# Soft mixture tail of a fused kernel: four-chunk logit blocks, squares on two engines, six weight buffers, a chain in halves

## Chip, cores and metric

One core of a Trainium2 chip runs the whole program once. The metric is device time in microseconds (us), the median over runs. Engines are named as the profile names them: PE does matrix multiplies, DVE, ACT and POOL work elementwise, SP issues the data transfers (DMA). All transfers of this kernel go through one queue, SP's.

## The reference, cut to what matters

```python
attn = clustered attention over q, k, v          # [4, 8, 768, 64], 16 clusters
x = attn rearranged to [3072, 512]               # tokens x model
h = x @ w_in                                     # 512 -> 2048
x = (h * cos(h)) @ w_out                         # 2048 -> 512
logits = x @ phi                                 # 32 slots, 8 experts x 4
d = softmax(logits, axis=0); slot_input = d.T @ x
for e in 8 experts:
    slot_out[e] = relu(slot_input[e] @ w1[e]) @ w2[e]     # w1 [8,512,1024], w2 [8,1024,512]
c = softmax(logits, axis=1); out = c @ slot_out  # [3072, 512]
```

The expert weights w1 and w2 are 16.8 MB each in float32, and the output is 6.3 MB.

## The kernel before

The program has three stages, written out in one fixed order; each engine works through its own list in that order.

**Attention** (up to about 505 us) is not touched.

**MLP loop.** The 3072 tokens are 24 tiles of 128. A tile has four chunks of 512 hidden columns, so there are 96 chunks (`NC_`); the last two tiles are interleaved, so that the four buffers of `w_in` (pool `wbig`) come free one by one. Iteration c of the loop issues, in this order: `hchunk(c)`, twelve matmuls into `h` (L138); `post2(c-2)`, a sine on ACT (L751), its square on DVE (L755) and the product `gg` on DVE (L756); `post1(c-1)`, a copy on ACT (L145) and two range-reduction steps on DVE (L146, L147); `gev(c-4)`, a copy of the transposed chunk on ACT (L768); `gtr(c-3)`, four transposes on PE (L763). `h` has three buffers, so `hchunk(c)` waits for the product `gg` of chunk c-3. In odd iterations PE also does `logit` for two chunks (`lp`, L786; w_out is folded into `phi` beforehand, as `wphi`). Once a tile is complete its logits are copied (`soft1`), summed and spread (`lf`, L802 and L804), and their running maximum is taken on DVE (L808, L809); ACT loads the exponential's table (L824), takes the exponentials and loads the sine's table again (shown at L751); later `dt` (L850) and `accp` (L862) add the tile's weighted sum to `acc`.

**Tail.** After chunk 95 come the last logits, maximum, exponentials, `accp` and `acc` (L871), then `acct` (transposes of `acc`), `si` (times w_out, tiles `wo0` and `wo1`, L983), `sit` (L990), `he` (first expert layer, `expert_in`, L1006), `htp` (transposes), `so` (second expert layer, `expert_out`, L1051), `fo` (the output, L1071) and ten output transfers (L1081). `ctstack` builds the combine weights `ctk` in the tail. `warm` issues matmuls on a tile of zeros whose result nobody reads.

**Weights.** w1 and w2 are cut into 16 pieces of 2.1 MB: 0 to 7 are w1, 8 to 15 are w2 (8 to 11 for output columns 0 to 255, 12 to 15 for the rest, so that each contiguous run of a w2 piece is 256 floats, 1 KB; of a w1 piece it is 4 KB). Pool `wk` has five buffers: `wo0`, `wo1` and pieces 0 to 2, loaded in the MLP loop at c = 28, 36 and 44. Pieces 3 to 6 go to the four `wbig` buffers as `w_in` is used up (c = 89, 91, 93, 95), piece 7 and part of piece 8 to pool `wx`, opened when the MLP's buffers are closed. The rest follows as buffers come free: second half of 9 after the first half of `si`, 10 after `si`, 11 to 15 each after one step of `expert_in`. A load that has to wait for its buffer holds up all transfers written behind it on SP.

Of the kernel before, what the change touches and what calls it, by code (L numbers as in the profile page):

```python
# [19 lines left out]
P = 128  # L20
# [6 lines left out]
def clustered_attention_then_soft_moe(  # L27
# [64 lines left out]
    R = {}  # L92
# [22 lines left out]
    def xprep2(t):  # L115
# [3 lines left out]
        lo = mx.tile([P, DT, P], F32R, tag="xlo", name=f"xlo{t}", bufs=3)  # L119
# [589 lines left out]
    wk = ctx.enter_context(tc.tile_pool(name="wk", bufs=5))  # L709
# [14 lines left out]
    def load_part(n, e, w):  # L724
        SP.dma_start(out=w if n < 8 else w.rearrange("p (t d) -> p t d", t=4), in_=piece(n)[:, e])
        W.setdefault(n, {})[e] = w

    def load_piece(n, pool, tag):
        w = pool.tile([P, 4, 1024], F32, tag=tag, name=f"w{n}")
        if n < 8:  # L730
            SP.dma_start(out=w, in_=piece(n))
            W[n] = [w[:, e] for e in range(4)]
        else:
            for e in range(4):
                load_part(n, e, w[:, e])

    with ExitStack() as m:
        mp = m.enter_context(tc.tile_pool(name="m2", bufs=2))
# [3 lines left out]
        zero = mp.tile([P, GRP * P], BF16, tag="zero", name="zero", bufs=1)  # L742
        POOL.memset(zero, 0.0)
        wo = [wk.tile([P, 8, DM], F32, tag="wk", name=f"wo{x}") for x in range(2)]

        def post2(c):
# [5 lines left out]
            if c == NC_ - 2:  # L752
# [36 lines left out]
        def soft1(ts):  # L789
            n = len(ts)  # L790
            lps = mp.tile([P, n * P], F32, tag="lps", name=f"lps{ts[0]}", bufs=1)
# [24 lines left out]
        def softx(ts):  # L816
# [5 lines left out]
            d = mp.tile([P, n * P], F32, tag="d", name=f"d{ts[0]}", bufs=1)  # L822
            e = mp.tile([P, n, NS], F32, tag="e", name=f"e{ts[0]}")
# [10 lines left out]
        def soft3(ts):  # L834
# [37 lines left out]

        xsched = {}
# [12 lines left out]
        WARM = {96: 2, 97: 2, 98: 2, 99: 4, 100: 12, 101: 8, 102: 4}  # L886
        for c in range(2, NC_ + 8):
            if c < NC_:
# [241 lines left out]
```

## Time and profile before

| what | value |
|---|---|
| median of 3 runs | 975.82 us (973.89 to 977.09) |
| the profiled execution's own time | 976.18 us |
| its span, first to last instruction | 974.5 us |
| PE busy, share of the span | 94% |
| DVE busy | 82% |
| ACT busy | 65% |
| POOL busy | 48% |

The span is what the trace's clock covers; the profiled execution's time is 1.7 us more. A busy share is an average over stages with different limits, so the stages have to be read apart.

### The profile page before, as it was taken

To read this page: it belongs to the slowest core of one execution; us is meant where nothing else is said; L and a number is where in the kernel's file an instruction comes from. 1 tells how busy PE (TensorE), PEld (TensorE's weight loads), DVE (VectorE), ACT (ScalarE), POOL (GpSimd) and SP (SyncE) were. 2 spreads that over 40 slices of the span, in tenths; PEclk is the share of its full clock that TensorE was granted. 3 is DMA by queue.
4 is the path that set the end of the run, shared out by engine and by line. 5 is a ranking of instruction groups with operands and counts; after the bars stand their busy time and mean duration, and the time that the engine had idled before them with its cause. 6 is when DMAs were issued, how large, how long until landed. Compare 5 with 4: busy or idle time off the path is not lost.

```text
span 974.5 us, 16981 instructions
## 1 busy us (share of the span) xinstructions
PE 915.4 (94%) x5974; PEld 622.9 (64%) x5974; DVE 796.1 (82%) x1577; ACT 633.8 (65%) x1368; POOL 464.1 (48%) x342
## 2 busy tenths in 40 slices
PE   5899999999999999999998999999999999999895
PEld 3466656666655666556666777777777777666443
DVE  6789999989989898899887888888888888777141
ACT  4687777777777777777554666666666666566232
POOL 3547877777777778777862222222222222220000
PEclk9999999999999999999999999999999999999998
DMA  8968766688666886666230224331301010127999
GB/s 174 210 166 191 189 157 176 163 205 194 141 178 161 197 193 148 173 159 175 80 97 29 65 88 130 109 100 54 130 23 44 23 44 23 43 89 283 352 349 332
DMA packets 138628, 142.18 MB, mean 146 GB/s; under 512 B 58376, under 2 KB 113968, under 8 KB 138544
## 3 DMA queue, kind: packets, MB, share of 16 engines
q1 hardware_dynamic: 138544, 141.11, 54.0%
q8 instruction: 47, 0.77, 0.3%
q14 instruction: 37, 0.30, 0.1%
HBM read 86.27 MB, written 17.06 MB: 106 GB/s over the span
## 4 chain that ended last, share of the span: by engine, by line
PE 63%; DVE 15%; DMA 9%; ACT 7%; issue 3%; SPq 1%; POOL 1%; ACTq 0%; POOLq 0%; DVEq 0%
PE h L138 19%; PE o L411 10%; PE sm L364 6%; PE s L398 5%; PE s L399 5%; DVE mc L366 3%; PE gt L763 3%; DMA mds<-mrow 2%; DVE kk L755 2%; PE accp L862 2%; DMA st<-mds 2%; DMA w<-in_moe_w_out_dram 2%; PE lp L786 2%; DVE w L469 2%; PE he L1006 1%
## 5 line engine op out<-in xcount | busy, mean ns | idle before, releaser
L138 PE MATMUL h<-wc,xhi 128*128 128x512 f32 x768 | 250.0, 406 | 8.5 <-DVE gg L756 8.5
L419 POOL TENSOR_TENSOR ps<-ps,a 128x768 f32<-128x768 f32 x120 | 230.8, 1923 | 43.9 <-ACT wphi L504 23.8
L366 DVE TENSOR_REDUCE mc<-sm 128x1 f32<-128x384 f32 x384 | 202.9, 549 | 33.6 <-PE sm L364 31.9
L402 ACT ACTIVATE a<-s 128x384 f32<-128x384 f32 x384 | 173.5, 490 | 37.5 <-PE s L399 32.4
L138 PEld LDWEIGHTS h<-wc,xhi 128*128 128x128 f32 x768 | 137.2, 188 | 62.7 <-DVE kk L147 17.3
L398 PE MATMUL s<-st 97*128 97x384 f32 x384 | 141.3, 368 | 11.4 <-DMA st<-mds 10.0
L138 PE MATMUL h<-wc,xlo 128*128 128x512 f32 x384 | 151.6, 395 | 0.0
L364 PE MATMUL sm<-st 96*128 96x384 f32 x384 | 140.4, 391 | 8.9 <-DVE mc L366 5.1
L411 PE MATMUL o<-a,vt 128*64 128x384 f32 x768 | 145.1, 499 | 0.0
L399 PE MATMUL s<-st 128*128 128x384 f32 x384 | 130.0, 339 | 0.0
L751 ACT ACTIVATE kk<-kk 128x512 f32<-128x512 f32 x96 | 60.6, 632 | 80.7 <-DVE kk L147 80.4
L364 PEld LDWEIGHTS sm<-st 96*128 96x128 f32 x384 | 72.7, 193 | 55.1 <-DVE mc L366 28.5
L755 DVE TENSOR_TENSOR kk<-kk 128x512 f32<-128x512 f32 x94 | 78.2, 832 | 29.8 <-ACT kk L751 29.7
L398 PEld LDWEIGHTS s<-st 97*128 97x128 f32 x384 | 73.0, 190 | 29.8 <-issue 13.9
L411 PEld LDWEIGHTS o<-a,vt 128*64 128x64 f32 x768 | 47.8, 136 | 61.0 <-issue 55.5
L109 POOL TENSOR_TENSOR xn<-xn,rc 128x512 f32<-128x512 f32 x24 | 31.9, 1328 | 107.7 <-DMA rc<-recs 104.7
L138 PEld LDWEIGHTS h<-wc,xlo 128*128 128x128 f32 x384 | 72.2, 188 | 17.0
L416 POOL TENSOR_TENSOR ps<-a,a 128x768 f32<-128x768 f32 x30 | 54.8, 1825 | 39.7 <-ACT a L402 39.0
L121 POOL TENSOR_TENSOR xlo<-xn,xhi 128x512 fp32r<-128x512 f32 x24 | 36.5, 1523 | 77.6 <-DVE xhi L120 77.6
L399 PEld LDWEIGHTS s<-st 128*128 128x128 f32 x384 | 73.1, 190 | 0.0
L113 POOL TENSOR_TENSOR xn<-xn,rc 128x512 f32<-128x512 f32 x24 | 32.3, 1345 | 81.2 <-DVE rc L111 76.1
L756 DVE SCALAR_TENSOR_TENSOR gg<-kk,h 128x512 f32<-128x512 f32 x96 | 65.9, 687 | 4.5 <-POOL kk L755 1.1
(203 smaller groups left out, 1567.0 us busy)
## 6 DMA issues: line engine op xcount, KB each, us to landing
w<-in_moe_w_dram SPq DMA_DIRECT2D x8, 2048.0 KB
st<-qhi SPq DMA_DIRECT2D x32, 384.0 KB
st<-khi SPq DMA_DIRECT2D x64, 192.0 KB
w<-in_moe_w_dram SPq DMA_DIRECT2D x24, 512.0 KB
w<-in_moe_w_out_dram SPq DMA_DIRECT2D x16, 512.0 KB
w<-in_moe_w_in_dram SPq DMA_DIRECT2D x16, 512.0 KB
qt<-in_q_dram SPq DMA_DIRECT2D x32, 192.0 KB
kt<-in_k_dram SPq DMA_DIRECT2D x32, 192.0 KB
```

The lines of the kernel that those rows point to most:

```text
L138: PE.matmul(h, lhsT=x[:, d, :], rhs=wc[f][:, w, d, :], start=(n == 0), stop=(n == 3 * DT - 1))
L364: PE.matmul(m[:, 0:QW], lhsT=st[0:96, Q1 + h, qt * P:(qt + 1) * P], rhs=st[0:96, K1 + h, half * QW:(half + 1) * QW], start=True, stop=True)
L366: DVE.tensor_reduce(out=s["mc"][:, col:col + 1], in_=m[:, 0:QW], op=ALU.max, axis=AX.X)
L398: PE.matmul(x[:, 0:QW], lhsT=st[0:97, K1 + h, ks], rhs=st[0:97, Q1 + h, qs], start=True, stop=False)
L399: PE.matmul(x[:, 0:QW], lhsT=st[:, K2 + h, ks], rhs=st[:, Q2 + h, qs], start=False, stop=True)
L402: ACT.activation(out=T[i][u][:, h, :], in_=x[:, 0:QW], func=AF.Exp, scale=scale)
L411: PE.matmul(s["o"][64 * h:64 * h + 64, 0:QW], lhsT=s["v"][:, h, kt, :], rhs=t[:, h, :], start=(kt == 0), stop=(kt == KT - 1))
L416: (DVE if i == NPAIR - 1 else POOL).tensor_tensor(out=ps, in0=s[u - 1], in1=t, op=ALU.add)
L419: (DVE if i == NPAIR - 1 else POOL).tensor_tensor(out=ps, in0=ps, in1=t, op=ALU.add)
L751: ACT.activation(out=r, in_=r, func=AF.Sin, scale=0.5)
L755: (POOL if c == NC_ - 3 else DVE).tensor_tensor(out=r, in0=r, in1=r, op=ALU.mult)
L756: DVE.scalar_tensor_tensor(out=R["g", t][:, f * 512:(f + 1) * 512], in0=r, scalar=0.5, in1=h, op0=ALU.subtract, op1=ALU.mult)
```

## The change

In the MLP loop the logits of a tile are now computed in one block of four chunks, in every fourth iteration; the copied chunks have four buffers for it (pool `gsp`). The square is taken on ACT for even chunks and stays on DVE for odd ones. The tile `xlo` has two buffers where it had three, and some small tiles share buffers.

Pool `wk` has six buffers, so pieces 0 to 3 are loaded inside the loop (c = 28, 36, 44, 52) and `wbig` takes pieces 4 to 7. Pieces 8 to 11 are cut otherwise: all 512 output columns of the first four experts, 256 rows each, in runs of 4 KB; 12 to 15 are as before. After the first half of `si` a buffer is loaded with the second half of piece 9 and the first of 10, and so on (`load_halves`).

The code from chunk 95 on is written out by hand. The last chunk's copy is on DVE; the sum for `acc` of tile 21 and the table load stand elsewhere; the two logit results have banks of their own; `accp`, `acc`, `acct`, `si` and `sit` are done in halves of 256 columns; `ctstack` is split into `ct_dve`, `ct_pe` and `ct_ev`, whose four blocks stand between the steps of this chain instead of between the steps of `expert_out`. The second group's transposes (`expert_tr(1)`) stand behind piece 11.

```diff
-        lo = mx.tile([P, DT, P], F32R, tag="xlo", name=f"xlo{t}", bufs=3)
+        lo = mx.tile([P, DT, P], F32R, tag="xlo", name=f"xlo{t}", bufs=2)
...
-    wk = ctx.enter_context(tc.tile_pool(name="wk", bufs=5))
+    wk = ctx.enter_context(tc.tile_pool(name="wk", bufs=6))
...
-        hf, g, fq = (n - 8) // 4, (n - 8) // 2 % 2, n % 2
-        return w2[4 * g:4 * g + 4, 512 * fq:512 * fq + 512, 256 * hf:256 * hf + 256].rearrange("e (p t) d -> p e t d", p=P)
+        if n < 12:
+            y = n - 8
+            return w2[0:4, 256 * y:256 * y + 256, :].rearrange("e (p t) d -> p e t d", p=P)
+        hf, fq = divmod(n - 12, 2)
...
+    def load_halves(n, w):
+        for e in range(2):
+            load_part(n, 2 + e, w[:, e])
+        if n < 15:
+            for e in range(2):
+                load_part(n + 1, e, w[:, 2 + e])
...
+        gs_stack = ExitStack()
+        gsp = gs_stack.enter_context(tc.tile_pool(name="gsp", bufs=4))
...
-            if c == NC_ - 2:
+            if c == NC_ - 2 or (c % 4 in (0, 2)):
                 ACT.activation(out=r, in_=r, func=AF.Square)
...
-        def gev(c):
-            s = mp.tile([P, 512], F32, tag="gts", name=f"gts{c}", bufs=2)
-            ACT.activation(out=s, in_=R.pop(("gp", c)), func=AF.Copy)
+        def gev(c, eng=None):
+            s = gsp.tile([P, 512], F32, tag="gts", name=f"gts{c}")
+            if eng is DVE:
+                DVE.tensor_copy(s, R.pop(("gp", c)))
+            else:
+                ACT.activation(out=s, in_=R.pop(("gp", c)), func=AF.Copy)
...
+        def ct_dve(b):
+            cs = spare[:, 0:4 * KT * NS].rearrange("p (t a b s) -> p t a b s", t=KT, a=2, b=2)
+            eb = ck[:, b * KT:b * KT + KT, :].rearrange("p t (o s) -> p t o s", o=1).to_broadcast([P, KT, 2, NS])
+            DVE.tensor_copy(cs[:, :, :, 0, :], eb)
+            DVE.tensor_tensor(out=cs[:, :, :, 1, :], in0=eb, in1=cs[:, :, :, 0, :], op=ALU.subtract)
+
+        def ct_pe(b):
+            cf = spare[:, 0:4 * KT * NS].rearrange("p (t s) -> p t s", t=KT).bitcast(F32)
+            for x in range(2):
+                g = psum.tile([P, 512], F32, tag=("m0", "m3")[x], name=f"ctk{b}_{x}")
+                for y in range(3):
+                    PE.transpose(g[:, y * P:(y + 1) * P], cf[:, 3 * x + y, :], ident)
+                R["ct", b, x] = g
+
+        def ct_ev(b):
+            for x in range(2):
+                ACT.activation(out=ctk[:, b * KT + 3 * x:b * KT + 3 * x + 3, :],
+                               in_=R.pop(("ct", b, x))[:, 0:3 * P].rearrange("p (t s) -> p t s", t=3), func=AF.Copy)
...
-        WARM = {96: 2, 97: 2, 98: 2, 99: 4, 100: 12, 101: 8, 102: 4}
...
-            if c % 2 == 1 or c - 4 == NC_ - 1:
-                for x in (c - 5, c - 4):
-                    if 0 <= x < NC_ and ("gt", x) in R:
-                        logit(x)
+            if c % 4 == 3:
+                for x in range(max(c - 7, 0), c - 3):
+                    logit(x)
...
-            if c in (28, 36, 44):
...
+            if c in (28, 36, 44, 52):
                 load_piece((c - 28) // 8, wk, "wk")
...
-                load_piece(NF - 1 - (NC_ - 1 - c) // GRP + 3, wbig, "wbig")
...
-                load_piece(7, wx, "wx")
...
+                load_piece(NF - 1 - (NC_ - 1 - c) // GRP + 4, wbig, "wbig")
+
+        last = groups[-1]
+        post1(NC_ - 1)
+        post2(NC_ - 2)
+        post2(NC_ - 1)
+        gev(NC_ - 4)
+        gtr(NC_ - 3)
+        gev(NC_ - 3)
+        gtr(NC_ - 2)
+        logit(NC_ - 4)
+        logit(NC_ - 3)
+        mx_stack.close()
+        wx = ctx.enter_context(tc.tile_pool(name="wx", bufs=1, side="right"))
+        w8 = wx.tile([P, 1024], F32, name="w8b")
+        load_part(8, 2, w8)
+        cbuf = wx.tile([P, 3840], F32R, name="cbuf")
+        ctk = cbuf[:, 0:NT * P].rearrange("p (t s) -> p t s", t=NT)
+        spare = cbuf[:, NT * P:]
+        gev(NC_ - 2)
+        ACT.activation(out=ones[:, 0:1], in_=ones[:, 0:1], func=AF.Exp)
+        gtr(NC_ - 1)
+        gev(NC_ - 1, DVE)
+        soft5([NT - GRP - 1])
+        ct_dve(0)
+        warm(2)
+        logit(NC_ - 2)
+        logit(NC_ - 1)
+        gs_stack.close()
+        w9 = ctx.enter_context(tc.tile_pool(name="tail", bufs=1)).tile([P, 2, 1024], F32, name="w9a")
+        for e in range(2):
+            load_part(9, e, w9[:, e])
+        lps = mp.tile([P, GRP * P], F32, tag="ld", name="lpsz", bufs=1)
+        ACT.activation(out=lps, in_=R["lpg"].rearrange("p a b -> p (a b)"), func=AF.Copy)
+        warm(4)
...
+        DVE.tensor_reduce(out=mn, in_=lf, op=ALU.max, axis=AX.X)
+        DVE.tensor_scalar(out=ng, in0=mn, scalar1=R["m"], scalar2=-1.0, op0=ALU.max, op1=ALU.mult)
+        DVE.tensor_reduce(out=rn, in_=lt, op=ALU.max, axis=AX.X)
+        DVE.tensor_scalar(out=rn, in0=rn, scalar1=-1.0, scalar2=None, op0=ALU.mult)
+        R["soft2"] = lf, lt, R["m"], ng, rn
+        softx(last)
+        ct_pe(0)
+        ct_dve(1)
+        soft3b(last)
+        softe(last)
+        soft3a(last)
+        DVE.tensor_scalar(out=ssum, in0=ssum, scalar1=1e-9, scalar2=None, op0=ALU.add)
+        DVE.reciprocal(ssum, ssum)
+        ct_ev(0)
+        cr, dts = R["dts"]
+        ap = [psum.tile([P, 256], F32, tag=("v", "m1")[h], name=f"apz{h}") for h in range(2)]
+        gz = [R.pop(("g", t)) for t in last]
+        for h in range(2):
+            for y in range(GRP):
+                for j in range(4):
+                    PE.matmul(ap[h][32 * j:32 * j + 32, :], lhsT=dts[:, y * P + 32 * j:y * P + 32 * j + 32],
+                              rhs=gz[y][:, j * 512 + 256 * h:j * 512 + 256 * h + 256], start=(y == 0), stop=(y == GRP - 1))
         gl = ggp.tile([P, 2, 1024], F32, tag="gg", name="gl")
         load_part(8, 3, gl[:, 0])
         htb = ggp.tile([P, 2, 8, P], F32, tag="gg", name="htb")
...
+        for h in range(2):
+            x = slice(256 * h, 256 * h + 256)
+            DVE.scalar_tensor_tensor(out=acc[:, x], in0=acc[:, x], scalar=cr, in1=ap[h], op0=ALU.mult, op1=ALU.add)
+            g = psum.tile([P, 512], F32, tag="s", name=f"acct{h}", bufs=3)[:, 0:256]
+            for j in range(2):
+                PE.transpose(g[:, j * P:(j + 1) * P], acc[:, 256 * h + j * P:256 * h + (j + 1) * P], ident)
+            ACT.activation(out=acct[:, 2 * h:2 * h + 2, :], in_=g.rearrange("p (a b) -> p a b", a=2), func=AF.Copy, scale=-2.0)
+            if h == 0:
+                ct_pe(1)
+        soft3c(last)
+        ct_ev(1)
+        ct_dve(2)
+        si = [psum.tile([P, 256], F32, tag=("m2", "m1")[h], name=f"si{h}") for h in range(2)]
+        for xh in range(2):
+            for h in range(2):
+                for x in range(2 * xh, 2 * xh + 2):
+                    for f in range(4):
+                        PE.matmul(si[h][32 * f:32 * f + 32, :], lhsT=acct[:, x, 32 * f:32 * f + 32],
+                                  rhs=wo[xh][:, 4 * (x - 2 * xh) + f, 256 * h:256 * h + 256], start=(x == 0), stop=(x == 3))
...
+        def sit_half(h):
+            ACT.activation(out=sis[:, 256 * h:256 * h + 256], in_=si[h], func=AF.Copy, scale=ssum)
+            g = psum.tile([P, 2 * NS], F32, tag="v", name=f"sit{h}")
+            for d in range(2):
+                PE.matmul(g[:, d * NS:(d + 1) * NS], lhsT=sis[:, (2 * h + d) * P:(2 * h + d + 1) * P], rhs=gmat[:, 0, :], start=True, stop=True)
+            ACT.activation(out=sit[:, 2 * h:2 * h + 2, :], in_=g.rearrange("p (a b) -> p a b", a=2), func=AF.Copy)
+
+        sit_half(0)
+        ct_pe(2)
+
+    if True:
+        for n in (9, 10):
+            load_halves(n, wk.tile([P, 4, 1024], F32, tag="wk", name=f"wh{n}"))
...
+                if n == 0:
+                    sit_half(1)
+                    ct_ev(2)
+                    ct_dve(3)
                 if n < 5:
-                    load_piece(11 + n, *pools[n])
+                    pool, tag = (wk, "wk") if n < 4 else (wbig, "wbig")
+                    load_halves(11 + n, pool.tile([P, 4, 1024], F32, tag=tag, name=f"wh{11 + n}"))
...
+        expert_ev(0)
+        expert_in(1)
+        ct_pe(3)
         expert_tr(0)
-        expert_in(1)
-        cbuf = wbig.tile([P, 4096], F32R, tag="wbig", name="cbuf")
-        ctk = cbuf[:, 0:NT * P].rearrange("p (t s) -> p t s", t=NT)
...
+            if n < 12:
+                steps = [(hf, 2 * (n - 8) + t, 512 * t + 256 * hf) for t in range(2) for hf in range(2)]
+            else:
+                hf, fq = divmod(n - 12, 2)
...
+        for n in range(8, 12):
+            expert_out(n)
+        expert_tr(1)
+        expert_out(12)
+        expert_out(13)
...
+                expert_out(14, [x // 3])
...
+        expert_out(15)
```

On PE, one tile's worth of the loop, with the twelve matmuls of each `hchunk` left out (`gt`: transposes of a chunk, `lp`: logits, `dt` and `accp`: the weighted sum of the tile before). Before:

```order
L763 MATMUL gt_6925<-ident,gg_6775 128x128 x4
L786 MATMUL lp_6930<-gts_6870,wphi 32x128 x4
L786 MATMUL lp_6930<-gts_6909,wphi 32x128 x4
...
L763 MATMUL gt_6970<-ident,gg_6775 128x128 x4
L850 MATMUL dt_6975<-ident,d_6914 128x128
...
L763 MATMUL gt_7006<-ident,gg_6952 128x128 x4
L786 MATMUL lp_6930<-gts_6960,wphi 32x128 x4
L786 MATMUL lp_6930<-gts_6999,wphi 32x128 x4
L862 MATMUL accp_7021<-gg_6613,dts_6977 32x512 x4
```

After:

```order
L771 MATMUL gt_6928<-ident,gg_6768 128x128 x4
...
L771 MATMUL gt_6964<-ident,gg_6768 128x128 x4
L868 MATMUL dt_6969<-ident,d_6917 128x128
...
L771 MATMUL gt_7000<-ident,gg_6946 128x128 x4
L797 MATMUL lp_7005<-gts_6872,wphi 32x128 x4
L797 MATMUL lp_7005<-gts_6912,wphi 32x128 x4
L797 MATMUL lp_7005<-gts_6954,wphi 32x128 x4
L797 MATMUL lp_7005<-gts_6993,wphi 32x128 x4
L880 MATMUL accp_7024<-gg_6606,dts_6971 32x512 x4
```

The eight `lp` instructions that stood alone two iterations ahead of `accp` now stand directly ahead of the other eight.

On SP, the transfers from the last w_in buffer's release to the outputs (`w_...` and `wh_...`: whole buffers; `w8a`, `w8b`, `gl`, `w9a`: half and quarter pieces in other tiles). Before:

```order
L731 DMA w_10294<-in_moe_w_dram 128x4x1024
L731 DMA w_10376<-in_moe_w_dram 128x4x1024
L731 DMA w_10464<-in_moe_w_dram 128x4x1024
L725 DMA w8a<-in_moe_w_dram 128x4x256 x2
L731 DMA w_10544<-in_moe_w_dram 128x4x1024
L731 DMA w_10590<-in_moe_w_dram 128x4x1024
L725 DMA w8b<-in_moe_w_dram 128x4x256
L725 DMA gl<-in_moe_w_dram 128x4x256
L725 DMA w9a<-in_moe_w_dram 128x4x256 x2
L725 DMA w9b<-in_moe_w_dram 128x4x256 x2
L725 DMA w_10734<-in_moe_w_dram 128x4x256 x4
```

After:

```order
L733 DMA w_10291<-in_moe_w_dram 128x4x1024
L733 DMA w_10382<-in_moe_w_dram 128x4x1024
L733 DMA w_10457<-in_moe_w_dram 128x4x1024
L728 DMA w8a<-in_moe_w_dram 128x1024 x2
L733 DMA w_10550<-in_moe_w_dram 128x4x1024
L728 DMA w8b<-in_moe_w_dram 128x1024
L728 DMA w9a<-in_moe_w_dram 128x1024 x2
L728 DMA gl<-in_moe_w_dram 128x1024
L728 DMA wh_10764<-in_moe_w_dram 128x1024 x4
L728 DMA wh_10769<-in_moe_w_dram 128x1024 x4
L728 DMA wh_10793<-in_moe_w_dram 128x1024 x2
L728 DMA wh_10793<-in_moe_w_dram 128x4x256 x2
```

One whole buffer (`w_10590`, piece 7 in `wx`) is gone from this stretch, `w9a` stands ahead of `gl`, and the loads of pieces 8 to 11 are one run of 1024 per partition instead of four of 256.

## Rows read from the trace of the kernel before

**Rows 1.** Stretches: us; each engine's busy us (instructions); granted PE clock; DMA share; GB/s.

```profile
554.90:893.60 338.70, 333.37 (x2266) 253.21 (x2262) 287.39 (x642) 217.74 (x439) 83.30 (x60) 1.00 0.25 80
893.60:917.40 23.80, 19.79 (x178) 11.68 (x178) 8.47 (x23) 10.45 (x25) 1.04 (x1) 1.00 0.99 354
917.40:957.40 40.00, 38.29 (x424) 18.74 (x424) 11.50 (x53) 13.41 (x26) 0.00 (x0) 1.00 1.09 349
957.40:974.50 17.10, 6.57 (x52) 4.42 (x52) 3.19 (x5) 4.84 (x10) 0.00 (x0) 0.82 0.93 320
```

**Rows 2.** Chain that ended last, in the MLP loop: start us, us, what.

```profile
554.07 0.86 PE accp L862 x8
...
577.95 0.57 PE lp L786 x16
578.53 2.98 PE h L138 x12
...
582.05 2.80 PE h L138 x12
...
585.86 0.86 PE accp L862 x8
...
892.59 1.00 PE accp L862 x8
```

**Rows 3.** Waits of PE, 505 to 897 us: us in total, times, longest.

```profile
PE h L138 <- DVE gg L756: 8.5, 14, 1.1
```

**Rows 4.** Chain that ended last, in a tile where PE waits.

```profile
660.90 1.08 DVE kk L755
```

**Rows 5.** Groups: the square on DVE: count, busy us, mean ns, idle before.

```profile
L755 DVE TENSOR_TENSOR kk<-kk 128x512 f32<-128x512 f32 x93 | 77.5, 834 | 29.8 <-ACT kk L751 29.7
```

**Rows 6.** ACT in order of time: a sine and its one square.

```profile
897.11 0.62 ACT L751 ACTIVATE kk<-kk 128x512 f32<-128x512 f32 x1
897.76 0.63 ACT L753 ACTIVATE kk<-kk 128x512 f32<-128x512 f32 x1
```

**Rows 7.** Chain that ended last, from the last logits to the first expert layer.

```profile
902.55 0.43 PE lpg L786 x8
...
904.55 2.18 PE warm L884 x20
...
907.42 1.97 PE accp L862 x16
...
909.41 0.75 DVE acc L871
...
911.56 3.69 PE si L983 x32
...
917.45 7.12 PE he L1006 x64
```

**Rows 8.** SP's transfers in order of time: start us, us until the last was issued.

```profile
896.61 5.00 SPq L731 DMA_DIRECT2D w<-in_moe_w_dram  x2
...
908.55 0.55 SPq L725 DMA_DIRECT2D gl<-in_moe_w_dram  x1
...
915.26 35.12 SPq L725 DMA_DIRECT2D w<-in_moe_w_dram  x24
```

**Rows 9.** Stretches as in rows 1, cut by which weights were on their way.

```profile
871.30:896.60 25.30, 24.89 (x172) 18.25 (x171) 17.43 (x40) 16.80 (x35) 1.04 (x1) 1.00 0.73 265
...
900.00:908.00 8.00, 6.99 (x80) 4.75 (x76) 2.38 (x9) 4.53 (x13) 0.00 (x0) 1.00 1.02 409
...
925.00:955.00 30.00, 29.02 (x341) 15.66 (x343) 11.50 (x53) 12.31 (x25) 0.00 (x0) 1.00 1.10 349
```

**Rows 10.** Chain that ended last: the last weight transfer.

```profile
948.96 8.47 DMA w<-in_moe_w_dram
```

**Rows 11.** PE in order of time: six transposes, early and a little later.

```profile
5.47 1.51 PE L249 MATMUL tpq<-ident,qt 128*128 128x128 f32 x6 [0.90 <-DMA qt<-in_q_dram]
...
35.38 0.85 PE L249 MATMUL tpk<-ident,kt 128*128 128x128 f32 x6 [0.54 <-DMA kt<-in_k_dram]
```

More of the change, by code (lines that the diff above doesn't have):

```diff
@@ L729, in load_piece @@
         w = pool.tile([P, 4, 1024], F32, tag=tag, name=f"w{n}")
[L730 to L735, printed above, removed]
+        SP.dma_start(out=w, in_=piece(n))
+        W[n] = [w[:, e] for e in range(4)]
+    def load_halves(n, w):
[4 more added lines that the diff above has]
+                load_part(n + 1, e, w[:, 2 + e])
     with ExitStack() as m:
-        mp = m.enter_context(tc.tile_pool(name="m2", bufs=2))
+        mp = ctx.enter_context(tc.tile_pool(name="m2", bufs=2))
         m0 = mp.tile([P, 1], F32, tag="mrun", name="mrun")
@@ L944, in clustered_attention_then_soft_moe @@
                 x = (c - 12) // 8
[L945 to L946 removed]
+                for y in range(2):
+                    SP.dma_start(out=wo[x][:, 4 * y:4 * y + 4], in_=wod.rearrange("(f y p) d -> y p f d", f=4, p=P)[2 * x + y])
+            if c in (28, 36, 44, 52):
                 load_piece((c - 28) // 8, wk, "wk")
[L948 removed]
+            if NC_ - GRP * NF <= c and (NC_ - 1 - c) % GRP == 0:
                 if c == NC_ - 1:
@@ L963, in clustered_attention_then_soft_moe @@
         htb = ggp.tile([P, 2, 8, P], F32, tag="gg", name="htb")
-    with ExitStack() as z:
-        tp = z.enter_context(tc.tile_pool(name="tail", bufs=1))
-        w9 = tp.tile([P, 2, 1024], F32, name="w9a")
-        for e in range(2):
-            load_part(9, e, w9[:, e])
-        pools = [(wk, "wk")] * 3 + [(wbig, "wbig")] * 2
-        DVE.tensor_scalar(out=ssum, in0=ssum, scalar1=1e-9, scalar2=None, op0=ALU.add)
-        DVE.reciprocal(ssum, ssum)
-        g = mbank("acct")
-        for j in range(4):
-            PE.transpose(g[:, j * P:(j + 1) * P], acc[:, j * P:(j + 1) * P], ident)
-        acct = wphi.rearrange("p a s -> p (a s)").rearrange("p (a b) -> p a b", a=4)
-        ACT.activation(out=acct, in_=g.rearrange("p (a b) -> p a b", a=4), func=AF.Copy, scale=-2.0)
-        g = mbank("si")
-        for f in range(4):
-            for j in range(4):
-                ft = 4 * f + j
-                PE.matmul(g[32 * j:32 * j + 32, :], lhsT=acct[:, j, 32 * f:32 * f + 32], rhs=wo[ft // 8][:, ft % 8, :],
-                          start=(f == 0), stop=(f == 3))
+        acct = wphi.rearrange("p a s -> p (a s)").rearrange("p (a b) -> p a b", a=4)
@@ L985, in clustered_attention_then_soft_moe @@
         hs = gl[:, 1]
         sis = hs[:, 0:512]
-        ACT.activation(out=sis, in_=g, func=AF.Copy, scale=ssum)
-        g = mbank("sit")
-        for d in range(DT):
-            PE.matmul(g[:, d * NS:(d + 1) * NS], lhsT=sis[:, d * P:(d + 1) * P], rhs=gmat[:, 0, :], start=True, stop=True)
         sit = phis
-        ACT.activation(out=sit, in_=g[:, 0:DT * NS].rearrange("p (a b) -> p a b", a=DT), func=AF.Copy)
-        w9 = wk.tile([P, 4, 1024], F32, tag="wk", name="w9b")
-        for e in range(2, 4):
-            load_part(9, e, w9[:, e])
```

120 lines of the change are left out of this document (47 added, 73 removed).

## Prediction

> **What bounds the kernel now.** I read the stretches first [rows 1]. In the MLP loop PE is busy 333 of 339 us, DVE 287 and ACT 218, while the transfers run at 80 GB/s: PE sets the pace there. From 893.6 us on it is the other way round: the transfers run at 354 and 349 GB/s with a DMA share of 0.99 and 1.09, up to the last weight, and the outputs follow at 320. So the end of the kernel is set by when the MLP loop ends and by how many bytes are still to move then, and at what rate.
>
> In the loop, the chain of waits [rows 2] runs over PE through most tiles: `h`, transposes, `lp`, `accp`. From the `accp` of tile 0 (554.07) to that of tile 21 (892.59, itself 0.14 us longer) 21 tiles take 338.5 us, 16.1 each. The tile between 570.0 and 585.86 has no wait in its chain and takes 15.87. The difference comes from waits: PE stands 8.5 us in all, 14 times, because `gg` of three chunks back is late [rows 3], always after the softmax of a tile, where two table loads hold up the sine; then the chain runs sine, square, `gg`, `h` (such a square in [rows 4]).
>
> In the tail, the chain goes through the engines, from the last logits at 902.55 to the first expert layer at 917.45 [rows 7], but SP is issuing weight loads without a pause from 915.26 for 35 us [rows 8], and the last weight takes 8.47 us from 948.96 to 957.4 [rows 10]. Shorter steps on PE would only bring earlier what is not waited for, except where a step gives back a buffer that a transfer waits for.
>
> **Four-chunk logit blocks.** A block of eight `lp` that stands alone costs more than itself: `lp` 0.57, and the `h` behind it takes 2.98 where one without a block ahead takes 2.80 [rows 2]. That is 0.75 us for the lone block. Joined to the other eight, ahead of `accp`, the same instructions should cost at most the row's 0.57; if the lead-in of the block is also shared, nearer 0.40. I take 0.57, so 0.18 us a tile, and for 22 tiles **-4 us** (to -7.7 with 0.40). The same sixteen `lp` are issued, in the same iteration as the tile's end, so the softmax behind them starts no later. The copied chunks now wait up to four iterations; four buffers cover that, and only the fifth copy waits for the block's first four instructions, a fraction of 0.57 us, on ACT, which is idle a third of the loop.
>
> Against it: the lone block stood just ahead of the `h` that waits for the late `gg`. Without it PE comes there 0.75 us earlier. If the softmax's chain does not shorten, PE waits up to that much in each tile, and what was saved at the block is spent there. That sets the bad end, below.
>
> **Squares on ACT.** DVE's square takes 834 ns in the mean of 93 [rows 5] and 1.08 in the tile shown [rows 4]; ACT's takes 0.63 and follows its sine at 897.11 + 0.62 within 0.03 us, with no table load between them [rows 6]. So 48 squares leave DVE, 40 us of its 287, and ACT takes on 48 times 0.63, 30 us on top of 218 of 339. ACT stays below DVE. The late `gg` after a softmax is that of an even chunk: its square shortens by 1.08 - 0.66 = 0.4 us in the tile shown, and 0.2 at the mean. In the iteration ahead the even square leaves DVE too, so sine, copy and the maximum's steps there come some 0.3 us sooner. Together 0.5 to 0.7 us against the 0.75 by which PE comes earlier: about even. I let the waits of 8.5 us shrink by **-2 us**; bounds: 0.55 us of new waits in each of 22 tiles, +12, and -5. Loop in all: **-6 us**, from +8 to -12.7.
>
> **One piece less behind the loop.** Piece 3 is now loaded at c = 52, where the transfers run at 80 GB/s; it delays nothing there, since the next tile's input is asked for three iterations later. Behind the loop there are 2.10 MB less. The rate for whole w1 pieces is 409 GB/s (900 to 908 us) [rows 9]: 2.10 / 0.409 = **-5.1 us**.
>
> **Runs of 4 KB.** The same view has 349 GB/s from 925 to 955 us, when only w2 pieces with runs of 1 KB are under way. I read the difference to 409 as that of the run length, since nothing else in the pieces differs. The rest of piece 8 and 9 to 11 are 7.3 MB in runs of 4 KB now: 21.0 us becomes 17.9, **-3.1 us**; 0 if the rate is due to something else. The Trainium skill would have it so: the page DMA: Bandwidth & Descriptors (Specifications) puts the smallest run for full rate at 512 B, which both lengths pass. By its rule this term is nothing, and the sum 3.1 us later; the trace, with two rates side by side, speaks against it.
>
> **A stop in the transfers.** By 896.6 us, when chunk 95's matmuls end, three w1 pieces and half of piece 8 are issued, 7.34 MB, of which 25.3 us at 265 GB/s have moved 6.7 [rows 9]. What can be loaded without a buffer of `si` is now, besides these 0.6 MB, piece 7 (2.1), and the rest of 8 and half of 9 (2.1): 4.8 MB, 11.8 us at 409, so the queue runs empty near 908.5. The next load waits for `wo0`, that is for the first half of `si`. Before, there were 2.1 MB more to bridge this, and `gl` and what follows came at 908.55 [rows 8]. Now the chain: the last product 0.7 earlier, as the 0.75 of `acc` [rows 7] is moved behind it; the last copy on DVE instead of behind the table load, and the maximum without waiting for the second logit result and with one step less, together 0.9 (an estimate; the bound is nothing); `accp` to `si` took 4.1 us and takes the 1.97 of `accp` plus half an `acc`, two transposes and a copy, less what the block of `ct_pe` adds (six transposes, about 0.8): some 3.5. So `si` starts near 909 and its first half (half of 3.69) ends near 910.7. The first bytes come a little later: the transfers stand still about 2.5 us: **+2.5 us**; bounds 0 and 6 (6 if the chain is not shortened at all).
>
> PE must not become late instead. `he` starts near 914 rather than at 917.45; two groups of `he` at 7.1 [rows 7], the transposes and four pieces of `so` come to about 939, while piece 11 lands near 926, and the pieces in runs of 1 KB follow six us apart (2.1 / 0.349) until about 950. So from piece 13 on PE waits for weights again. The four `ct` blocks fill waits of PE ahead of `he`; in the old place they stood among the `so`.
>
> **The sum.** Tail -5.1 - 3.1 + 2.5 = -5.7; loop -6; together -11.7. The span goes from 974.5, where the last stretch of [rows 1] ends, to 962.8. The profiled execution's own time is 1.7 us above its span, so 964.5; it is 0.4 above the median of the runs, so **964 us**.
>
> **The rivals.**
> (1) *The transfers give less*: the run length does nothing (+3.1) and the stop is 5 to 6 us (+3): 970. For it: the two rates come from different stretches. Against it: each is steady over its stretch.
> (2) *The softmax becomes the loop*: PE only arrives earlier and waits: the loop gives +8 instead of -6, with the tail's -5.7: 978 at the bound, 974 with half of the new waits. For it: 14 of 22 tiles already have such a wait [rows 3]. Against it: the shorter square.
> (3) *More than that*: the joined block shares its lead-in (-3.7), most of the 8.5 us go (-3), no stop (-2.5): 955 to 957.
> (4) *Slower, by the clock*: the change takes out most of the idle-work matmuls in the chain (20 of them in 2.18 us [rows 7] were one of seven groups; two groups of 2 and 4 stay). PE at half its clock is in this trace: six transposes take 1.51 us early on and 0.85 us at 35 us [rows 11]. If the clock falls from 2.4 to 1.2 GHz in the chain and stays there through `he` and `so`, about 32 us of matmuls take 64, and the end comes near 995. It decides from about 12 us of such lengthening on, which is what the rest gains. Against it: the granted clock is 1.00 in every stretch up to 957 [rows 1], and the new chain leaves no wait of PE above 1 us. The Trainium skill speaks for it: the page TensorE: Matmul & The Clock Gate (Part 4: PE-mode transpose) says that transposes do not count as PE being busy in the way that matmuls do, and the fill-in work is now transposes. No row here shows whether they do.
> (5) *It does not do what it says*: loads that wait elsewhere on SP bring back the old order of transfers, and the loop stays as it was: 974 to 977.
>
> **How the numbers follow.** Forecast, 960 to 967: 0.53. Rival 1: 0.20. Rival 2: 0.07. Rival 3: 0.11. Rival 4: 0.05. Rival 5: 0.04. A measurement of this kernel can tell about 0.3%, 3 us, from no change. The first, second and fourth of these cases lie below 973; with half of rival 2 that makes 0.87 faster, 0.07 the same, 0.06 slower. The range from 955 to 972 leaves out the slower rivals and the outer part of the third.
>
> **What would show it.** The time from tile 0's `accp` to tile 21's falls from 338.5 to about 334, with no `h` behind a lone `lp`; the wait of `h` for `gg` falls below 8.5 us in total. In the 15 us behind the first `si` the transfers run near 409 GB/s, then 349; between, a dip of 2 to 3 us ahead of the first whole `wh` load. The last weight lands about 55 us after the end of chunk 95's matmuls instead of 60.8. The prediction is wrong if the `lp` block of sixteen costs as much as two, if the new `h` wait eats it, if the dip is above 6 us, or if the granted clock is below 1 between the loop's end and the last `so`.

## The result and the profile after

The changed kernel takes 964.57 us (median of 4 runs, 962.48 to 965.77), the kernel before beside it 976.33 (973.89 to 977.09): a ratio of 0.9866, 95% interval 0.9829 to 0.9902. A second time, on the chip of the experiments, it was 964.9 against 977.62 (0.9876, 0.9826 to 0.9925). Predicted were 964 us.

The profiled run took 962.48 us, its span is 960.7, 13.8 less than before. The stretches, with the columns of [rows 1]; the cut at 886.86 is the end of chunk 95's `h`, which was at 896.6 before:

```profile
552.62:882.80 330.18, 326.34 (x2249) 253.32 (x2241) 244.43 (x597) 242.74 (x480) 83.11 (x60) 1.00 0.27 87
882.80:886.86 4.06, 4.06 (x22) 2.65 (x23) 2.81 (x8) 1.61 (x3) 1.04 (x1) 1.00 1.03 399
886.86:898.00 11.14, 9.16 (x134) 6.10 (x134) 8.13 (x20) 8.25 (x20) 0.00 (x0) 1.00 0.98 373
...
898.00:901.55 3.55, 3.55 (x58) 2.29 (x54) 2.01 (x8) 1.53 (x4) 0.00 (x0) 1.00 0.50 160
901.55:903.00 1.45, 1.45 (x32) 0.76 (x24) 0.00 (x0) 0.47 (x1) 0.00 (x0) 1.00 0.50 54
903.00:908.00 5.00, 5.00 (x47) 2.44 (x46) 0.92 (x2) 1.58 (x5) 0.00 (x0) 1.00 0.89 266
908.00:918.00 10.00, 10.00 (x97) 2.99 (x93) 0.00 (x0) 1.38 (x2) 0.00 (x0) 1.00 1.02 408
...
918.00:943.20 25.20, 22.56 (x288) 13.19 (x284) 2.70 (x5) 8.54 (x17) 0.00 (x0) 1.00 1.09 351
943.20:960.70 17.50, 6.53 (x59) 4.40 (x58) 3.70 (x6) 5.50 (x12) 0.00 (x0) 0.79 0.95 324
```

DVE gives up 43 us in the loop (from 287 in [rows 1]) and ACT takes on 25; PE stays the one that sets the pace. Of the 13.8 us, 8.5 are gained between the `accp` of tile 0 and that of tile 21 (338.63 before, counted from PE's own first row, now 330.18), and 4.1 from the end of chunk 95's `h` to the end of the span (77.9, now 73.8). The other 1.2 lie in the opening, and are no effect that can be told from chance: in the twelve other runs below, whose attention is the same code as after's, tile 0's `accp` starts anywhere from 546.9 to 558.0. So stretches are compared below, not only times.

One tile of the loop in the chain that ended last, in answer to [rows 2]:

```profile
568.42 0.86 PE accp L880 x8
...
583.04 1.01 PE lp L797 x32
584.05 0.86 PE accp L880 x8
```

15.63 us for a tile without a wait, where it was 15.87: 0.24 us for the joined block. The waits of PE inside the loop, before and then after (in all, times, longest). [Rows 3] begins at 505 us, and 3.6 of its 8.5 us turn out to lie ahead of tile 0's `accp`:

```profile
PE h L138 <- DVE gg L756: 4.9, 10, 1.0
```

```profile
PE h L138 <- DVE gg L764: 2.9, 5, 1.3
```

SP's transfers behind the loop, in answer to [rows 8]:

```profile
892.99 0.80 SPq L728 DMA_DIRECT2D w9a<-in_moe_w_dram  x2
898.01 0.33 SPq L728 DMA_DIRECT2D gl<-in_moe_w_dram  x1
901.55 34.26 SPq L728 DMA_DIRECT2D wh<-in_moe_w_dram  x26
939.46 13.98 SPq L1165 DMA_DIRECT2D out_dram<-ob  x10
```

`gl` waits for `accp`'s buffer until 898.01 and the first `wh` load for the first half of `si` until 901.55, and in between the transfers thin out: 160 GB/s up to there, 54 until 903, 266 until 908, together 1.98 MB or 198 GB/s, and then 408. The chain, in answer to [rows 7, 10]:

```profile
896.45 1.93 PE apz L1037 x32
...
899.63 3.59 PE si L1060 x64
...
906.88 7.05 PE he L1088 x64
...
928.33 8.89 DMA wh<-in_moe_w_dram
937.25 0.62 PE so L1135 x2
...
943.20 1.91 PE so L1135 x32
```

`si` starts 12.8 us after the end of chunk 95's `h` (15.0 before). The load waited for at 937.25 is not the last: four of 0.52 MB follow it, 1.5 us each at 349 GB/s, so the last weight comes at about 943.2 (an estimate from those rows), 56.3 us after chunk 95's `h` instead of 60.8.

### The profile page after: what moved, and what is told of

Same layout as the page of the kernel before. It is cut to its first block, busy times and chain, and to the rows that moved or that the text cites. A ratio compares the mean times of both kernels' runs of the same rounds, so it can differ in the third digit from the quotient of the medians.

```text
span 960.7 us, 16962 instructions
## 1 busy us (share of the span) xinstructions
PE 907.7 (94%) x5994; PEld 625.5 (65%) x5994; DVE 749.8 (78%) x1491; ACT 662.3 (69%) x1417; POOL 462.8 (48%) x342
## 3 DMA queue, kind: packets, MB, share of 16 engines
q1 hardware_dynamic: 132432, 141.11, 54.5%
## 4 chain that ended last, share of the span: by engine, by line
PE 66%; DVE 13%; ACT 8%; DMA 7%; issue 2%; SPq 2%; POOL 0%; ACTq 0%; POOLq 0%
PE h L138 22%; PE o L411 10%; PE sm L364 6%; PE s L398 5%; PE s L399 4%; DVE mc L366 4%; PE gt L771 3%; DMA w<-in_moe_w_out_dram 3%; DVE w L469 2%; PE lp L797 2%; PE accp L880 2%; DMA mds<-mrow 2%; SPq L728 1%; ACT L759 1%; ACT L835 1%
## 5 line engine op out<-in xcount | busy, mean ns | idle before, releaser
L147 DVE SCALAR_TENSOR_TENSOR kk<-kk,h 128x512 f32<-128x512 f32 x96 | 66.0, 688 | 3.3
```

The lines of the kernel that those rows point to most:

```text
L147: DVE.scalar_tensor_tensor(out=a, in0=a, scalar=-TWO_PI, in1=h, op0=ALU.mult, op1=ALU.add)
```

## The experiments

Loop: from PE's first row of tile 0's `accp` to the row of tile 21's; waits: `h` for `gg` inside it; tail: from the end of chunk 95's `h` to the end of the span. All in us, from each kernel's profiled run; ratios are to the kernel before on the same chip.

| kernel | time, median | ratio, 95% | loop | waits | tail |
|---|---|---|---|---|---|
| before | 976.33 | 1 | 338.6 | 4.9 | 77.9 |
| after | 964.57 | 0.983 to 0.990 | 330.2 | 2.9 | 73.8 |
| after, again | 964.9 | 0.983 to 0.993 | 330.6 | 3.2 | 75.8 |
| squares on DVE | 977.1 | 0.997 to 1.001 | 342.2 | 12.8 | 74.5 |
| two-chunk blocks | 968.15 | 0.988 to 0.993 | 332.5 | 1.0 | 73.9 |
| both undone | 974.25 | 0.994 to 0.997 | 339.4 | 5.4 | 73.7 |
| all squares on ACT | 966.38 | 0.986 to 0.993 | 332.6 | 3.6 | 74.5 |
| runs of 1 KB | 967.28 | 0.984 to 0.994 | 331.9 | 4.3 | 75.6 |
| without wo1 | 958.02 | 0.975 to 0.986 | 331.1 | 3.8 | 71.3 |
| bridge | 963.61 | 0.981 to 0.990 | 331.4 | 4.0 | 75.3 |
| bridge in gg | 961.97 | 0.981 to 0.988 | 331.7 | 4.2 | 71.5 |
| bridge, filled | 962.42 | 0.979 to 0.987 | 332.1 | 4.2 | 71.8 |
| bridge, so steps | 960.69 | 0.979 to 0.987 | 331.4 | 4.1 | 70.6 |
| 100 transposes | 972.31 (one) | - | 330.9 | 3.3 | 83.9 |

The nine traces with after's loop give 330.2 to 332.1 (mean 331.2), so the change is worth 7.4 us there rather than the 8.5 of its own trace, and a difference of 1 to 2 us between two single traces says little by itself. The six traces with after's tail (the first six rows below the kernel before) give 73.7 to 74.5, and once 75.8.

**Squares back on DVE.**

```diff
-            if c == NC_ - 2 or (c % 4 in (0, 2)):
+            if c == NC_ - 2:
```

> The changed kernel with all squares of the loop back on DVE (but that of chunk 94, as before); the four-chunk logit blocks stay. In the two traces the loop from tile 0's accp to tile 21's went from 338.5 to 330.0 us: a tile in which PE does not wait went from 15.87 to 15.63, 21 of them 5.0 us, and 3.4 us are left for waits of h for gg (8.5 us in all before, 4.9 after). Theory, the prediction's: the square on ACT acts through those waits alone. A tile without a wait stays at 15.63, the waits return to 8.5 us or somewhat more, since PE comes 0.24 us earlier: loop 333 to 337, time 968 to 972. Rival 1 (the new wait eats the block's saving): waits of 13 us and more, loop 338 or above, time 973 or above. Rival 2 (the squares do nothing, the waits fell for another reason): loop 330, time 964 to 965.

**Two-chunk blocks.**

```diff
-            if c % 4 == 3:
-                for x in range(max(c - 7, 0), c - 3):
+            if c % 2 == 1:
+                for x in range(max(c - 5, 0), c - 3):
```

> The changed kernel with the logits of a tile in two blocks of two chunks again; the squares of even chunks stay on ACT. Theory: a tile without a wait returns to 15.87, so 21 tiles cost 5.0 us more, and the waits stay near 4.9 us or below: loop 334 to 335.5, time 969 to 970.5. Rival 1 (the prediction's sizes: 0.18 a tile for the block): loop 333.8. Rival 2 (the block gave nothing, the shorter tile comes from the squares): a tile without a wait stays at 15.63, loop 330, time 964 to 965.

**Both.**

> The changed kernel with both loop edits undone: two-chunk blocks and squares on DVE; tail, six weight buffers and smaller buffers as in the changed kernel. Theory: the loop is that of the kernel before, 338.5 us from tile 0's accp to tile 21's and 8.5 us of waits, and what is left is the tail's: the stretch from chunk 95's last h to the end was 77.9 us before and 73.8 after; the span then ends near 969, the time near 971. Rival: the smaller buffers (xlo with two, ld shared) or the moved weight loads have part in the loop's gain: loop 333 to 336 and time 966 to 968; or they cost something that the two edits hide: loop above 340.

The waits of `h` for `gg` in these three, in this order, each from its own trace:

```profile
PE h L138 <- DVE gg L764: 12.8, 21, 1.6
```

```profile
PE h L138 <- DVE gg L764: 1.0, 2, 0.5
```

```profile
PE h L138 <- DVE gg L764: 5.4, 10, 0.9
```

With both undone the loop is before's within 0.8 us: the smaller buffers and the moved loads have no part in it that one trace could show. The two edits are not a sum. The joined block alone lengthens the loop by 2.7 us (339.45 to 342.17; the times, 974.25 and 977.1 on one chip, agree): its instructions give back 21 times 0.24 = 5.0, and PE then waits in 21 places, 7.4 us more, which was rival 1 of this run and rival 2 of the prediction. The squares alone shorten it by 7.0 (339.45 to 332.45), 4.4 of it in listed waits. The rest is in the same waits, of which a list shows only the part behind the end of the row before. PE in order of time, first with the squares alone, where `h` has its `gg`, then with both undone:

```profile
569.28 0.27 PE L868 MATMUL dt<-ident,d 128*128 128x128 f32 x1
569.31 0.71 PE L138 MATMUL h<-wc,xhi 128*128 128x512 f32 x2
```

```profile
646.81 0.27 PE L868 MATMUL dt<-ident,d 128*128 128x128 f32 x1
647.73 0.72 PE L138 MATMUL h<-wc,xhi 128*128 128x512 f32 x2 [0.65 <-DVE gg L764]
```

`h` starts 0.92 us behind `dt` where 0.03 is enough, so it is 0.89 us late and 0.65 are listed. Summed over the starts of PE's rows in this way, `h` is late by 8.8 us with both undone and by 2.4 with the squares alone, 6.3 of the 7.0 (and by 18.1 with the squares on DVE, 6.0 in after). On top of the squares the block brings 1.2 to 2.3 in the loop, little more than traces of one loop differ by. Where the time goes without the squares is in the chain that ended last, in one tile of the run with the squares on DVE:

```profile
645.53 1.28 ACT L835
...
647.76 1.28 ACT L759
...
649.05 0.64 ACT kk L759
...
649.72 1.06 DVE kk L763
...
650.81 0.70 DVE gg L764
...
651.55 3.06 PE h L138 x12
```

Two table loads of 1.28 us around the exponentials, then sine, square and `gg`, and PE stands until `gg` is there. The square there takes 1.06 us; on ACT it takes 0.63 [rows 6].

**All squares on ACT.**

```diff
-            if c == NC_ - 2 or (c % 4 in (0, 2)):
+            if c != NC_ - 3:
```

> The changed kernel with the squares of odd chunks on ACT too (all of the loop but chunk 93's, which is POOL's). Some 46 more squares of 0.63 us are 29 us on ACT (243 of 331 us busy in the changed kernel) and 38 us less on DVE (245). Theory from the four combinations (no square on ACT: 13.7 us of waits of h for gg with four-chunk blocks, half of them on ACT: 2.9 to 3.2): the waits come from the chain sine, square, gg behind the exponentials, and it is the even chunk's square that counts there; the odd chunks' squares on ACT stand in front of copies and sines that are waited for, so nothing more is gained: loop and waits within 1 us of the changed kernel's, time 963.5 to 966. Rival 1 (DVE's load as such makes gg late): waits fall to 1 us, loop 2 us shorter, time 962 to 963. Rival 2 (ACT is too full after a softmax): waits above 6 us, time 968 or above.

As expected by the theory: no gain, waits of 3.6 us, and 966.38 just outside the range given. Taking still more off DVE, at ACT's cost, does not bring `gg` sooner; what DVE's load alone would do, with ACT's unchanged, was not tried.

**Runs of 1 KB.** Pieces 8 to 11 are again 512 rows by 256 columns, in as many transfers of the same size.

```diff
-            return w2[0:4, 256 * y:256 * y + 256, :].rearrange("e (p t) d -> p e t d", p=P)
+            fq, hf = divmod(n - 8, 2)
+            return w2[0:4, 512 * fq:512 * fq + 512, 256 * hf:256 * hf + 256].rearrange("e (p t) d -> p e t d", p=P)
```

> The changed kernel with pieces 8 to 11 cut in runs of 256 floats (1 KB), as many bytes and as many transfers in the same order; nothing else differs. Theory, the prediction's: the rate of these pieces falls from 409 to 349 GB/s. In the changed kernel about 5.2 MB of them move when nothing but the rate limits them: 5.2/0.349 - 5.2/0.409 = 2.2 us; the time becomes 966 to 967.5, and the stretch from 908 to 918 us shows about 349 GB/s instead of 408. Rival: the rate of 408 is due to something else than the run length (the place in memory, the time in the program): no difference, 964 to 965, and 400 GB/s or more in that stretch. The Trainium skill, page DMA: Bandwidth & Descriptors (Specifications), puts full rate at runs of 512 B and above, which is the rival's side.

The ten us behind the stop, as in the windows of after:

```profile
911.90:921.90 10.00, 10.00 (x97) 2.99 (x93) 0.00 (x0) 1.38 (x2) 0.00 (x0) 1.00 1.09 354
```

354 GB/s where after has 408, with nothing changed but how the pieces are cut; the tail is 1.8 us longer than the first trace's of after and the time 2.4 to 2.7. The rate is settled; the size in the tail is less so: 75.6 lies 1.1 to 1.9 above five of the six traces with after's tail, but the sixth, after's second, has 75.8 too. The Trainium skill (DMA: Bandwidth & Descriptors, Specifications) counts both lengths as full rate; the two rows contradict it.

**Without wo1.** The second half of the table is not loaded and `si` reads the first half twice. So one buffer is free for the next half pieces, which no longer wait for `si`.

```diff
-        wo = [wk.tile([P, 8, DM], F32, tag="wk", name=f"wo{x}") for x in range(2)]
+        wo = [wk.tile([P, 8, DM], F32, tag="wk", name="wo0")] * 2
...
             load_part(9, e, w9[:, e])
+        load_halves(9, wk.tile([P, 4, 1024], F32, tag="wk", name="wh9"))
```

> Leaves out the second half of the table wo: wo1 is not loaded and si reads wo0 twice, so the output is not the reference's. The buffer that is free in this way takes the next half pieces (wh9) before si instead of after it. Theory: between 898 and 908 us 1.98 MB moved where 4.1 would have; with 2.1 MB more to load the transfers run on to about 903, when all of si is done and the next buffer is free, so most of the lost 5.1 us is given back, as far as PE follows: PE reaches piece 14 at 934.3 and its weights come at 937.25, so 3 to 4.5 us, time 960 to 961.5. Rival 1 (the stop costs nothing, since PE or the outputs set the end): 964 to 965. Rival 2 (the slow 5 us behind the stop, 263 GB/s from 903 to 908, are not due to the stop): they come again, and 2 to 3 us are gained.

The window around `si`, and the chain that ended last:

```profile
893.00:903.00 10.00, 10.00 (x128) 5.56 (x124) 3.12 (x10) 3.48 (x10) 0.00 (x0) 1.00 1.01 392
```

```profile
916.20 7.11 PE so L1136 x128
...
924.68 3.71 PE so L1136 x64
...
935.95 1.91 PE so L1136 x32
...
942.51 2.06 ACT ob L1160 x4
```

392 GB/s where after has 198, so the stop is gone, and the slow transfers behind it too (rival 2 is out). But only 2.5 us come back of some 5: no DMA stands in the chain behind the loop. PE goes from `he` through `so` to the output without a wait for a weight and sets the end. (The time, 958.02, is below the range given. The opening of the profiled execution ended at 546.9, the earliest of all; those of the other three were not traced, so the tail is what counts.)

**Bridges over the stop, with nothing left out.** First `ctk`'s buffer leaves `wx`, four quarter pieces go there, and the `ct` blocks move from the chain to between the `so` steps.

> A version that is to end the stop with the right output: ctk's buffer (15 KB a partition) is no longer in wx, so wx takes two quarter pieces of 8 and two of 9, the tail pool the rest of 9, and gl one quarter of 10; the ct blocks move from the chain ahead of si to between the steps of so, in a w1 buffer that he has given back. 2.1 MB more are on their way without waiting for si, and all later loads come into wo0, wo1 and pieces 0 to 3, each after one step of he. Theory: the stop of 5.1 us is gone but for about 1 us, the transfers run at about 409 GB/s until the 1 KB pieces; PE, which has the same work, reaches piece 14 at about 934 and limits the gain: 3 to 4 us, time 960 to 962. Rival 1: the four ct blocks between the so steps make PE late by another 2 us (0.7 each): 962 to 964. Rival 2 (the stop costs nothing): 964 to 965.

Second, the `ct` blocks stay; the second half of piece 9 goes into the `gg` buffer of `htb`, and `htb` into a w1 buffer.

```diff
-        htb = ggp.tile([P, 2, 8, P], F32, tag="gg", name="htb")
+        w9 = ggp.tile([P, 2, 1024], F32, tag="gg", name="w9b")
+        for e in range(2):
+            load_part(9, 2 + e, w9[:, e])
...
+        htb = wbig.tile([P, 4, 1024], F32, tag="wbig", name="htb")[:, 0:2].rearrange("p g (f d) -> p g f d", f=8)
```

> The changed kernel with 1.05 MB more of weights on their way ahead of si, and the right output: the second half of piece 9 goes into the gg buffer that htb had, htb goes into a w1 buffer that he has given back; pieces 10 to 15 then fill wo0, wo1 and pieces 0 to 3 whole. PE's order is untouched, the ct blocks stay in the chain. Theory (PE sets the end as soon as the weights are there): from the end of chunk 95's h to the span's end the changed kernel took 73.8 and 75.8 us, the run without wo1, in which PE waits for no weight, 71.3; here PE should wait for no weight either, so 71.3 to 72.5, time 961 to 962.5. Rival 1 (the bytes set the end and the stop's 5.1 us count in full): 1.4 us of stop are left, 70 to 70.5. Rival 2 (no gain, as in the run bridge): 73.8 to 75.8.

The first gains nothing (75.3). Its transfers run on past the place of the stop (402 GB/s from 893 to 903 us, then a dip to 293 until 908), but with the `ct` blocks gone PE waited in the chain, and the clock fell. PE in order of time, then the granted clock (last but two) in the stretch ahead and in `apz`:

```profile
897.67 3.28 PE L1028 MATMUL apz<-gg,dts 128*32 128x256 f32 x32 [0.47 <-ACT dts L867]
```

```profile
893.50:897.60 4.10, 2.43 (x20) 1.57 (x20) 2.26 (x9) 1.87 (x8) 0.00 (x0) 1.00 1.00 385
897.60:901.00 3.40, 3.33 (x33) 1.49 (x34) 0.48 (x2) 0.56 (x5) 0.00 (x0) 0.57 1.02 412
```

`apz` took 1.93 us in after and takes 3.28; and the four blocks now stand where PE sets the end. The second gains what the theory said, 71.5. Two kernels then fill PE's waits behind piece 13, one by `so` steps and `fo`, one by `so` steps alone (the lines below stand in both).

```diff
-        regroup(0)
+        regroup(0, lambda: expert_out(11, [0], [1]))
+        expert_out(11, [1], [1])
```

> The run bridge_gg with PE's order changed behind piece 13: four of so's steps for the second half of the columns (piece 11) are done while PE waits for sor and fo of the first half, and three fo of the first half while it waits for those of the second. PE waits 2.0 us there in the changed kernel (sor 1.1, fo 0.9). Theory (PE sets the end): 1.5 to 2 us less than bridge_gg, 69.5 to 70.8 us from chunk 95's h to the end, time 959.5 to 961. Rival (the output transfers set the end): the same time as bridge_gg, since the fourth part of the first half's output is issued 4 us later and the transfers run idle for that long: no gain or 1 to 2 us lost.

> The run bridge_gg with only the first half of bridge_fill: two of so's steps (piece 11, second half of the columns) each stand in front of sor and fo of the first half, where PE waits; the fourth part of the first half's output is not held back. From the end of chunk 95's h to the span's end bridge_gg took 71.5 us and bridge_fill 71.8; the first fo of the second half came 0.9 us sooner in bridge_fill, but the transfers ran at 295 GB/s for 5 us where they run at 349. Theory (PE's last steps set the end as long as the output transfers do not run dry): 70.5 to 71 us, time 960.5 to 962. Rival (the transfers of weights and output set it, PE no more): 71.5 to 72.

In one trace each, holding back the fourth part of the first half's output eats what the filling gains (71.8, the rival); without that it is 70.6, as the theory had it. The last of them, at 960.69 us, is the fastest kernel here that computes all of the reference; its interval (0.979 to 0.987) overlaps that of after (0.983 to 0.990), and it is by its tail, 3.2 to 5.2 us shorter in the traces, that it is told from it.

**100 transposes.**

```diff
+        for y in range(100):
+            PE.transpose(g[:, (y % 4) * P:(y % 4 + 1) * P], ident, ident)
         si = [psum.tile([P, 256], F32, tag=("m2", "m1")[h], name=f"si{h}") for h in range(2)]
```

> The changed kernel with 100 more transposes of a constant, whose results nobody reads, ahead of si. Six transposes take 0.69 us in the chain, so 100 take 11.3 us. Theory: every us by which si comes later, the first load into wo0 comes later, the transfers stand still that much longer, and the end comes 11 us later (span 972), since the transfers set it; the granted clock stays at 1.00 through the transposes and he behind them. Rival 1 (the end is not set by that stop): span 961 to 966. Rival 2 (transposes do not keep the clock up): the granted clock falls to 0.50 in the stretch of the transposes or behind it, 64 matmuls of he take 14 us instead of 7.05, and the span ends near 985 or later. The Trainium skill, page TensorE: Matmul & The Clock Gate (Part 4: PE-mode transpose), has transposes not count as activity of PE, which is rival 2.

PE in order of time, and the stretch with its granted clock:

```profile
899.15 11.08 PE L1057 MATMUL idle_tr<-ident 128*128 128x128 f32 x100
...
917.42 12.22 PE L1091 MATMUL he<-w,phis 128*32 128x512 f32 x112
```

```profile
898.70:910.10 11.40, 11.40 (x106) 11.29 (x104) 1.38 (x6) 1.31 (x4) 0.00 (x0) 1.00 0.12 47
```

11.08 us of transposes alone leave the granted clock at 1.00, and 112 matmuls of `he` behind them take 12.22 us, as in after's own trace. The tail is 8 to 10 us longer, near the 11 put in. So transposes hold the clock here, against the Trainium skill's page TensorE: Matmul & The Clock Gate (Part 4: PE-mode transpose) as the prediction read it. Whether they would also raise it from its lower level was not tried.

The same trace has a longer stop in the transfers than after's, and it bears on what comes behind a stop. The first `wh` load is issued at 912.16 (901.55 in after). The stretch ahead of it, and the five us from 1.45 us behind it on, which in after are 903 to 908:

```profile
901.00:912.16 11.16, 11.16 (x125) 10.22 (x127) 0.00 (x0) 0.00 (x0) 0.00 (x0) 1.00 0.01 1
913.61:918.61 5.00, 5.00 (x46) 2.44 (x46) 0.92 (x2) 1.58 (x5) 0.00 (x0) 1.00 0.98 374
```

374 GB/s where after has 266: an empty queue as such does not make the transfers slow afterwards.

## Why the prediction was right, step by step

**The time** came out as predicted (964), the sum of two terms that were both off: the loop gained more than predicted, the tail less. That they cancel to within 1 us is luck.

**Loop, -6.** Measured -8.5 in the trace of after and -7.4 over nine traces. The total is near; read as what each edit is worth, the split (blocks -4, squares -2) is wrong. The block's own saving was sized well (0.18 us a tile predicted, 0.24 measured), and so was the shorter chain: from the start of a tile's `accp` to the end of the `gg` that the softmax holds up, 21 tiles take 12.36 us in the mean with the squares on DVE and 11.71 in after, 0.65 less, where 0.5 to 0.7 were predicted. But the step "for 22 tiles -4 us" took it as the block's worth. Alone it costs 2.7 us, and the objection that the prediction made itself, that PE only comes earlier to a `gg` that is late, is what happens. The squares, taken as "about even", carry the loop: 7.0 us alone, 11 on top of the block. That step failed because it weighed the shorter square only against the block's earlier arrival, and not against the waits that are there without it. That "I let the waits of 8.5 us shrink" also rested on a window that began before the loop; inside it there were 4.9 to win.

**One piece less, -5.1.** From chunk 95's `h` to the end 24.7 MB move (73.84 us at 335 GB/s) instead of 27.0 (77.9 at 346): 2.2 MB, 5.4 us at 409.

**Runs of 4 KB, -3.1.** The mechanism is shown (408 against 354 GB/s), the size is nearer 2: the share of these pieces that moved ahead of and inside the stop was not limited by the rate.

**A stop, +2.5.** Mis-sized; its bound of 6 held. Between 898 and 908 us 1.98 MB moved, where 4.09 would at 408: 5.2 us. The times in the chain were nearly right (queue dry 11.1 us after chunk 95's `h`, 11.9 predicted; `si`'s first half done at 14.6, 14.1 predicted). Left out was that the transfers do not come back at once: behind the load issued at 901.55 they stay at 54 GB/s until 903 and at 266 until 908 (311 in those five us of after's second trace).

**Tail, -5.7.** Measured -4.1 (73.8), with 75.8 in the second trace and 73.7 to 74.5 in the four other kernels with this tail. The last weight came at 56.3 (about 55 predicted, 60.8 before), and behind it the end took 17.5 us (17.1).

**PE "must not become late".** It nearly is. The prediction had PE wait for weights from piece 13 on; after waits 1.7 us in all, for piece 14. Transfers and PE set the end almost together, which is why taking the whole stop away gives 2.3 to 2.5 us and not 5.

**The rivals.** Rival 1 was half true (the stop near 5, the run length real). Rival 2 is what the block does without the squares. Rival 3 needed no stop. Rival 4 is out in the profiled run, with a clock of 1.00 to 943 us; the second trace of after shows a small one, in which the clock is 0.58 in the mean of 3.7 us while PE does the first outputs (0.50, its lower level, from 937.7 to 940.9), after a stretch in which it waited for weights:

```profile
935.60:937.90 2.30, 1.29 (x5) 0.30 (x5) 0.00 (x0) 0.00 (x0) 0.00 (x0) 0.94 1.09 352
937.90:941.60 3.70, 3.70 (x21) 2.55 (x20) 0.80 (x2) 1.54 (x3) 0.00 (x0) 0.58 0.60 193
```

The transfers run at 193 GB/s there because the outputs come late, and that makes most of the 2 us between the two tails. It is not all the clock's doing: counted from the end of chunk 95's `h`, the weight for piece 14 is there 1.2 us later than in the first trace (51.6 against 50.4) before the clock falls, and the first output is issued 1.9 us later (54.5 against 52.6). Rival 5 is out.

Left open: what holds the transfers at 266 GB/s for five us behind the stop. The empty queue alone does not (374 with 100 transposes), and nothing else was tried by itself.

## What to carry to other kernels

A saving on the engine that sets the pace is worth nothing by itself if that engine already waits for a chain after it: shorten the chain first (here the square, 1.06 to 0.63 us), then take the engine's own saving. In a tail that moves bytes, follow both the transfers and the compute engine to the first output, since the one hides what the other gains. Undo edits one by one and together: four kernels showed what the sum hid.

## What the runs showed that was not expected

In after a stop of the transfers cost more than its idle time: from 903 to 908 us, with loads issued, the rate was 266 GB/s and not the 408 that followed; yet behind the three times longer stop of the run with 100 transposes it was 374. The granted clock fell to 0.50, the lower of its two levels (1.2 and 2.4 GHz), for some 3.4 us after PE had been busy 2.43 of 4.10 us in the first bridge kernel and 1.29 of 2.30 in after's second trace. Two waits of nearly the same length in after's first trace (0.77 and 0.90 us for piece 14, where the second has 0.79 and 0.87) left it at 1.00; the second trace has one more, of 0.59 us, some four us ahead of them. And the opening of this program, the same code in all, ends anywhere within 11 us.
